# Fused attention and mixer layers on one core: one step of the float64 weight decoding moved from VectorE to ScalarE, with another order of the first 1000 pieces

## The chip, the cores and the metric

One core of one Trainium2 chip. The metric is device time in microseconds (us) of one execution of the whole program; lower is better. A core has TensorE (matrix products, into PSUM), VectorE, ScalarE and GpSimd (elementwise work) and SyncE, which here issues all transfers. Each engine takes its instructions in the order in which they were written and waits by itself for what they need. In the profile's rows TensorE is PE (its weight loads PEld), VectorE DVE, ScalarE ACT, GpSimd POOL, SyncE SP.

## What is computed

Three layers in a row, on a batch of 4 with 576 positions and 8 heads of 64 channels:

```
q_d, k_d, v_d = means over 4 positions               # 144 pooled positions
out = repeat(softmax(q_d k_d^T / 8) v_d, 4)          # pooled attention
    + softmax(band(q k^T / 8, |i - j| < 4)) v        # local attention
x = out as (4, 576, 512)

h = relu(x @ w_in)                                   # 512 -> 1024
c = sum over k of conv_w[k] * h shifted by k - 1
x = (h * sigmoid(c)) @ w_out                         # 1024 -> 512

u = x + ((x^T @ U) @ V)^T                            # along the positions, rank 32
y = u + relu(u @ w_ch1) @ w_ch2                      # 512 -> 2048 -> 512
```

The activations and q, k, v are float32. The weights (`w_in`, `conv_w`, `w_out`, `U`, `V`, `w_ch1`, `w_ch2`) arrive as float64, since numpy scales them with a float64 factor. They are read as pairs of 32-bit words and decoded on the chip.

## The kernel before, in words

The program is one list of some 2900 words, `SEQ`. Each word names a piece of work and its indices ("S.3.2": scores of pair 3 in PSUM slot 2), `ACTS` maps the name to a function, and the last loop of the kernel runs the list from left to right. Nothing else sets the order: every engine's queue is the list with the other engines' work left out, and SyncE's transfers stand in it too.

The stages overlap. The 16 pairs of (two heads) of attention are the words up to about 1060: sums over four positions (`sums`, L357), scores (L396, L462), maxima, exponentials, row sums, norms, transposes and the products with v (L530, L538), then `add_x` (L557). At the same time the 16 tiles of the first layer's weights are loaded and decoded, and the first layer starts: `g1` (L721), `relu1`, `conv_first`, `conv_rest` (L748), `tanh`, `gate` (L759), `gate_hi` and `gate_lo` (ghl, L764 and L767), `g2` (L775). The second layer's rank-32 mixing follows (L799, L820). The last layer multiplies with seven products per block of two by two (`product`, L927): `p_copy` (L932) and `p_add` (L936) bring the sums of PSUM banks together, `relu3_hi` and `relu3_lo` (L943, L947) split the result in two parts for `g4` (L959). `p_copy` reads a bank to which the next product of the block adds, so that product waits for it. The pieces "f" and the ones that `scores` adds issue matmuls whose result nobody reads (`beat`, L332).

A weight tile is 128 x 512 values, 128 x 1024 words. `w_load` brings it, `w_dec` decodes it in four steps, written as "wd.layer.tile.step" and placed in the list one by one. `dec` (L577) has the steps. With `hi` and `lo` the two words of each value (every second word of the tile) and `d` the 32 bits of the float32 that is made:

- step 0, ScalarE, L585: the high word read as a float32 and multiplied by 2^-112, into `wval`;
- step 1, VectorE, L587: `d` shifted left by 3;
- step 2, VectorE, L589: the low word shifted right by 29 (its upper three bits), or `d`;
- step 3, VectorE, L592: the sign bit of the high word, or `d`.

Then `w_hi` (ScalarE, L605) and `w_lo` (GpSimd or VectorE, L608) split the value in two reduced-precision parts for TensorE; the last layer makes sums of halves of `wval` instead (L849, L861, L865). The same `dec` decodes the convolution's weights (`cw`, 24 values a row) and U and V (`uvr`). 48 tiles are decoded: 16 of the first layer between 22 and 109 us, 32 of the last between 279 and 441 us.

Of the kernel before, what the change touches and what calls it, by code (L numbers as in the profile page):

```python
# [11 lines left out]
AF = mybir.ActivationFunctionType  # L12
ALU = mybir.AluOpType
# [5 lines left out]
SEQ = ("lq.1 xz sf sp.1 k sp.0 K qs.1 sp.1 S.1.1 lc cw.0 z M.1 lq.0 qs.0 qd.1 Sd.1.0 dp.1 lr.0 E.1 R.1 S.0.2 M.0 vs.0.0 "  # L19
# [196 lines left out]
P = 128  # L216
# [4 lines left out]
def mixer_kernel(ctx, tc, consts, qk, vw_, vr_, w1, w2, cw_, u_, v_, out):  # L221
    nc = tc.nc
    B, S, DM = out.shape
    NCC = DM // P
    NPAIR = qk.shape[0]
    D = P // 2
# [12 lines left out]
    Z = 2 if w1.dtype == U64 else 1  # L239
# [11 lines left out]
    px = tc.alloc_tile_pool(name="px", bufs=1, side="right", reuse_waits="tile")  # L251
# [325 lines left out]
    def dec(raw, dst, step, eng=nc.vector):  # L577
# [5 lines left out]
        d = dst.bitcast(U32)  # L583
# [483 lines left out]
```

## Time and profile before

| | |
|---|---|
| runs, us | 720.1, 720.26, 720.46; median 720.26 |
| the profiled execution | 715.93 us, span of its instructions 714.1 us |
| PE busy | 695.5 us (97%), 5809 matmuls |
| DVE busy | 450.7 us (63%), 790 instructions |
| ACT busy | 353.3 us (49%), 811 instructions |
| POOL busy | 207.1 us (29%), 209 instructions |
| mean granted clock of TensorE | 0.994 |
| transfers | 96.42 MB, mean 135 GB/s |

The profiled execution is one run of its own; its time is 4.3 us below the median of the others, and its rows add up to its own time. Busy is the union of an engine's instructions over the span; a busy TensorE is not TensorE at its peak, since matmuls are pipelined. A share over the whole span is a mean over stages that are bound by different things, so the stretches are read one by one. The granted clock is the share of full speed that TensorE was given.

### The profile page before, as it was taken

Reading aid. Unit: us, or ns where it says so; the run is one execution under the profiler, and the core shown is the slowest. Engines: PE = TensorE matmul, PEld = TensorE weight load, DVE = VectorE, ACT = ScalarE, POOL = GpSimd, SP = SyncE. Lnnn points to the kernel's source line nnn. Section 1 sums busy time; section 2 is a strip of 40 time slices with the busy share of each in tenths; the row PEclk is TensorE's granted clock in tenths of the full one; section 3 lists DMA queues with packets and bytes.
Section 4 is the critical chain, followed back from the end, with each engine's and each line's share of the span. In section 5 each row is a group of like instructions: output and inputs, shape, how many; then the busy total and the mean of one; then the engine's idle time right before and its main releaser. Section 6 shows DMA issues by size and latency. Waiting matters only on the chain.

```text
span 714.1 us, 14638 instructions
## 1 busy us (share of the span) xinstructions
PE 695.5 (97%) x5809; PEld 616.3 (86%) x5809; DVE 450.7 (63%) x790; ACT 353.3 (49%) x811; POOL 207.1 (29%) x209
## 2 busy tenths in 40 slices
PE   8888999999999999999999999999999999999997
PEld 6677879888889898988899988888898989998896
DVE  5999998867666466899899888832222273222223
ACT  4776877665457466787455555521221262221221
POOL 2366555444523454383332334200000020000000
PEclk9999999999999999999999999999999999999999
DMA  7988542221100000245666858454334426344312
GB/s 213 312 272 293 158 138 68 73 79 57 41 2 1 1 0 30 92 160 207 233 224 222 280 172 286 158 147 122 114 108 133 105 75 220 118 133 118 104 44 89
DMA packets 40579, 96.42 MB, mean 135 GB/s; under 512 B 4672, under 2 KB 5184, under 8 KB 40512
## 3 DMA queue, kind: packets, MB, share of 16 engines
q1 hardware_dynamic: 40512, 95.50, 41.8%
q8 instruction: 46, 0.75, 0.4%
q14 instruction: 21, 0.17, 0.1%
HBM read 76.08 MB, written 19.40 MB: 134 GB/s over the span
## 4 chain that ended last, share of the span: by engine, by line
PE 86%; DVE 9%; DMA 2%; issue 1%; ACT 1%; SPq 0%; POOL 0%; DVEq 0%; ACTq 0%
PE acc L959 26%; PE g L927 25%; PE g L721 14%; PE acc L775 13%; DMA vr<-in_vr_dram 2%; DVE wval L589 1%; PE h L799 1%; PE O L530 1%; DVE wval L592 1%; PE S L396 1%; PE O L538 1%; PE Sd L462 1%; PE Td L503 1%; PE mx L820 1%; DVE g L748 1%
## 5 line engine op out<-in xcount | busy, mean ns | idle before, releaser
L959 PE MATMUL acc<-w,a 128*128 128x512 f32 x864 | 218.6, 393 | 0.0
L927 PE MATMUL g<-bt,as 128*128 128x384 f32 x1008 | 194.7, 338 | 0.0
L927 PEld LDWEIGHTS g<-bt,as 128*128 128x128 f32 x1008 | 178.9, 188 | 10.5 <-ACT tp L932 0.7
L959 PEld LDWEIGHTS acc<-w,a 128*128 128x128 f32 x864 | 159.9, 188 | 26.2
L721 PE MATMUL g<-xhl,w 128*128 128x386 f32 (+1 forms) x576 | 117.5, 347 | 3.2 <-DVE ghl L767 3.2
L775 PE MATMUL acc<-w,ghl 128*128 128x512 f32 x432 | 112.1, 396 | 0.0
L721 PEld LDWEIGHTS g<-xhl,w 128*128 128x128 f32 x576 | 102.6, 191 | 8.6 <-DVE ghl L767 3.9
L936 DVE TENSOR_TENSOR tp<-g,tp 128x384 f32<-128x384 f32 x72 | 40.0, 556 | 100.6 <-ACT tp L932 61.7
L775 PEld LDWEIGHTS acc<-w,ghl 128*128 128x128 f32 x432 | 79.4, 188 | 14.3 <-issue 0.6
L932 ACT ACTIVATE tp<-g 128x384 f32<-128x384 f32 x72 | 35.2, 489 | 96.1 <-PE g L927 96.1
L943 ACT ACTIVATE a<-tp 128x384 fp32r<-128x384 f32 x72 | 37.7, 525 | 81.2 <-PE acc L959 57.5
L947 DVE SCALAR_TENSOR_TENSOR a<-tp,a 128x384 fp32r<-128x384 f32 x72 | 41.8, 581 | 56.6 <-ACT a L943 56.0
L748 DVE SCALAR_TENSOR_TENSOR g<-h,cw,g 128x384 f32<-128x384 f32 x96 | 59.4, 619 | 22.5 <-ACT g L743 21.1
L767 POOL TENSOR_TENSOR ghl<-ct,ghl 128x384 fp32r<-128x384 f32 x40 | 41.6, 1041 | 64.3 <-ACT ghl L764 64.3
L916 POOL TENSOR_TENSOR bt<-vb,bt 128x384 fp32r<-128x384 f32 x13 | 13.3, 1028 | 141.4 <-ACT bt L912 136.9
L608 POOL TENSOR_TENSOR w<-wval,w 128x512 fp32r<-128x512 f32 x26 | 34.6, 1332 | 57.4 <-ACT w L605 57.4
L589 DVE SCALAR_TENSOR_TENSOR wval<-raw,wval 128x512 uint32<-128x512 uint32 x48 | 38.5, 801 | 0.8
L592 DVE SCALAR_TENSOR_TENSOR wval<-raw,wval 128x512 uint32<-128x512 uint32 x48 | 37.7, 790 | 0.8
L764 ACT ACTIVATE ghl<-ct 128x384 fp32r<-128x384 f32 x40 | 20.9, 522 | 27.3 <-PE acc L775 25.0
L727 ACT ACTIVATE h<-g 128x386 f32<-128x386 f32 (+1 forms) x48 | 23.6, 491 | 21.7 <-PE g L721 21.6
L943 ACT ACTIVATE a<-g 128x384 fp32r<-128x384 f32 x24 | 11.8, 492 | 42.0 <-PE acc L959 29.9
L585 ACT ACTIVATE wval<-raw 128x512 f32<-128x512 f32 x48 | 31.5, 666 | 1.1 <-DVE w L608 1.0
(129 smaller groups left out, 849.8 us busy)
## 6 DMA issues: line engine op xcount, KB each, us to landing
as<-s SPq DMA_DIRECT2D x112, 256.0 KB, 2.7
raw<-in_w_dram SPq DMA_DIRECT2D x48, 512.0 KB, 4.9
s<-as SPq DMA_DIRECT2D x56, 256.0 KB, 2.9
qk<-in_qk_dram SPq DMA_DIRECT2D x16, 576.0 KB, 5.4
vw<-in_vw_dram SPq DMA_DIRECT2D x16, 384.0 KB, 5.0
vr<-in_vr_dram SPq DMA_DIRECT2D x16, 288.0 KB
out_dram<-u SPq DMA_DIRECT2D x17, 256.0 KB, 3.6
uvr<-in_v_dram SPq DMA_DIRECT2D x1, 576.0 KB
```

Source lines behind the costliest of these rows:

```text
L589: eng.scalar_tensor_tensor(out=d, in0=lo, scalar=29, in1=d, op0=ALU.logical_shift_right, op1=ALU.bitwise_or)
L592: eng.scalar_tensor_tensor(out=d, in0=hi, scalar=0x80000000, in1=d, op0=ALU.bitwise_and, op1=ALU.bitwise_or)
L721: nc.tensor.matmul(gp[n][:, :wd], w[:, a, cc], xhl[g, cc][:, b, :wd], start=cc == 0 and i == 0, stop=cc == NCC - 1 and i == 2)
L748: nc.vector.scalar_tensor_tensor(out=o, in0=inner(g, hts[n], k), scalar=cw[:, k * NF + f:k * NF + f + 1], in1=o, op0=ALU.mult, op1=ALU.add)
L767: eng.tensor_tensor(ghl[n][:, 1], cts.pop(n), ghl[n][:, 0].bitcast(F32), op=ALU.subtract)
L775: nc.tensor.matmul(acc[g][c], t[:, a, c * P:(c + 1) * P], w[:, b], start=f == 0 and i == 0, stop=f == NF - 1 and i == 2)
L927: nc.tensor.matmul(o, w[:, a, k], Bs[r, j, k][:, b, :TB], start=j in (0, 1, 3) and n == 0, stop=n == 3 * HC - 1, skip_group_check=True)
L932: nc.scalar.activation(out=t[:, :TB], in_=bank[q, 0][:, :TB], func=AF.Copy)
L936: nc.vector.tensor_tensor(t, bank[q, 1][:, :TB], t, op=ALU.add)
L943: nc.scalar.activation(out=t[:, 0], in_=r_src(q, k), func=AF.Relu)
L947: nc.vector.scalar_tensor_tensor(out=t[:, 1], in0=r_src(q, k), scalar=0.0, in1=t[:, 0].bitcast(F32), op0=ALU.max, op1=ALU.subtract)
L959: nc.tensor.matmul(acc2[g][c], t[:, a, c * P:(c + 1) * P], w[:, b], start=f == 0 and n < 2 and i == 0, stop=f == NFP - 1 and n >= 2 and i ...
```

## The change

`dec` makes the three bits of the low word on ScalarE: step 1 becomes an ACTIVATE in place on the low words, read as integers, scaled by 2^-29 (a little less) and shifted by -0.5 (a little more), and rounded to an integer as it is written. Step 2 on VectorE then shifts `d` by 3 and ors the three bits in one instruction. So a tile has two ScalarE and two VectorE steps, where it had one and three.

```diff
@@ dec @@
         if step == 0:
             nc.scalar.activation(out=dst, in_=hi.bitcast(F32), func=AF.Copy, scale=2.0 ** -112)
         elif step == 1:
-            eng.tensor_scalar(out=d, in0=d, scalar1=3, scalar2=None, op0=ALU.logical_shift_left)
+            nc.scalar.activation(out=lo, in_=lo, func=AF.Copy, scale=2.0 ** -29 * (1 - 2.0 ** -18),
+                                 bias=-0.5 + 7.5 * 2.0 ** -18)
         elif step == 2:
-            eng.scalar_tensor_tensor(out=d, in0=lo, scalar=29, in1=d,
-                                           op0=ALU.logical_shift_right, op1=ALU.bitwise_or)
+            eng.scalar_tensor_tensor(out=d, in0=d, scalar=3, in1=lo,
+                                     op0=ALU.logical_shift_left, op1=ALU.bitwise_or)
@@ SEQ @@
-SEQ = ("lq.1 xz sf sp.1 k sp.0 K qs.1 sp.1 S.1.1 lc cw.0 z M.1 lq.0 qs.0 qd.1 Sd.1.0 dp.1 lr.0 E.1 R.1 S.0.2 M.0 vs.0.0 "
+SEQ = ("lq.1 sf sp.0 sp.1 sp.1 k K lq.0 S.1.1 M.1 lq.2 S.0.2 z wm qs.1 qd.1 Sd.1.0 qs.0 qd.0 lc dp.1 E.1 M.0 dp.0 Sd.0.1 "
...
```

The list holds the same 2928 words. The first 1000 stand in another order; the 1928 behind them (from "re.15 r.15 Vd.14" on, in the middle of the first layer) are the same, word for word, and the step 1 of the last layer's 32 tiles keeps its places in the list, now in ScalarE's queue. In the changed file the lines up to `dec` are one lower (L584 is step 0 there, L586 the new step 1, L589 and L592 are steps 2 and 3).

VectorE at the first weight tile, before (`wval` is the decoded tile, `raw` the words, `nm`, `sm` and `P` belong to attention):

```order
L467 TENSOR_REDUCE nm<-Sd 96x3
L587 TENSOR_SCALAR wval<-wval 128x512
L589 SCALAR_TENSOR_TENSOR wval<-raw,wval 128x512
L411 TENSOR_REDUCE nm<-S 128x12
L592 SCALAR_TENSOR_TENSOR wval<-raw,wval 128x512
L450 RECIPROCAL sm_104<-sm_104 128x15
L418 TENSOR_TENSOR P<-S,nm 128x2x3x64
```

and with the change:

```order
L466 TENSOR_REDUCE nm<-Sd 96x3
L589 SCALAR_TENSOR_TENSOR cw<-cw,craw 128x24
L440 TENSOR_REDUCE sm_104<-P 128x12
L589 SCALAR_TENSOR_TENSOR wval<-wval,raw 128x512
L592 SCALAR_TENSOR_TENSOR wval<-raw,wval 128x512
L449 RECIPROCAL sm_104<-sm_104 128x15
```

The shift of L587 is gone, and a row sum of attention and a step of `cw` stand ahead of the tile's two steps.

ScalarE in the last layer, in the part of the list that is unchanged, where three tiles are decoded between the copies of `tp` (L932, `p_copy`; `a` is L943, `relu3_hi`):

```order
-L585 ACTIVATE wval_5375<-raw_5294 128x512
-L585 ACTIVATE wval_5381<-raw_5319 128x512
+L584 ACTIVATE wval_5375<-raw_5294 128x512
+L584 ACTIVATE wval_5381<-raw_5319 128x512
+L586 ACTIVATE raw_5294<-raw_5294 128x512
 L932 ACTIVATE tp_5387<-g_5368 128x384
-L585 ACTIVATE wval_5395<-raw_5325 128x512
+L586 ACTIVATE raw_5319<-raw_5319 128x512
+L584 ACTIVATE wval_5395<-raw_5325 128x512
 L943 ACTIVATE a_5404<-tp_5387 128x384
+L586 ACTIVATE raw_5325<-raw_5325 128x512
 L932 ACTIVATE tp_5415<-g_5368 128x384
```

Two ACTIVATEs more stand ahead of L943, and three ahead of the second `tp`.

## Rows read from the trace of the kernel before

**Rows 1.** The page: the chain of waits, shares of the span by engine.
```profile
PE 86%; DVE 9%; DMA 2%; issue 1%; ACT 1%; SPq 0%; POOL 0%; DVEq 0%; ACTq 0%
```

**Rows 2.** Windows: stretch, length, busy PE, PEld, DVE, ACT, POOL (instructions), clock, DMA, GB/s.
```profile
0.00:20.00 20.00, 17.03 (x401) 12.72 (x401) 12.66 (x23) 9.57 (x30) 5.99 (x16) 1.00 0.77 215
20.00:65.00 45.00, 36.69 (x784) 32.66 (x778) 43.29 (x72) 31.58 (x90) 22.24 (x19) 0.92 0.88 290
65.00:85.00 20.00, 20.00 (x303) 17.60 (x301) 17.10 (x30) 17.07 (x41) 11.33 (x11) 1.00 0.71 227
85.00:105.00 20.00, 18.34 (x328) 15.25 (x327) 19.79 (x35) 14.22 (x34) 10.96 (x10) 1.00 0.43 121
105.00:440.00 335.00, 335.00 (x2661) 299.36 (x2659) 261.65 (x459) 206.91 (x467) 146.04 (x146) 1.00 0.33 113
440.00:705.00 265.00, 263.75 (x1327) 235.12 (x1327) 91.95 (x169) 73.40 (x151) 10.48 (x10) 1.00 0.41 123
705.00:714.10 9.10, 4.70 (x21) 3.57 (x19) 4.23 (x8) 0.52 (x1) 0.00 (x0) 0.92 0.48 173
```

**Rows 3.** Timeline of TensorE: start, length, what, and idle time before.
```profile
29.05 1.06 PE L332 MATMUL O<-mask,identR 128*128 128x224 f32 x7 [2.83 <-DVE xd L548]
...
60.50 1.87 PE L721 MATMUL g<-xhl,w 128*128 128x386 f32 x5 [2.73 <-DVE ghl L767]
```

**Rows 4.** Windows of 5 us behind these two idle times.
```profile
30.00:35.00 5.00, 4.70 (x150) 4.17 (x152) 4.33 (x9) 4.11 (x11) 0.20 (x1) 0.67 0.94 287
60.00:65.00 5.00, 4.50 (x16) 4.33 (x17) 5.00 (x11) 2.44 (x6) 2.05 (x2) 0.66 0.94 280
```

**Rows 5.** Chain of waits to 125 us: start, length, what.
```profile
23.19 0.42 DVE wval L587
...
32.28 0.68 ACT wval L585
...
40.09 1.56 DVE wval L587 x2
...
60.50 3.93 PE g L721 x12
...
91.27 0.34 DVE wval L587
...
121.67 2.15 PE g L721 x12
```

**Rows 6.** Groups of instructions from 20 to 105 us: busy us, mean ns, idle.
```profile
L589 DVE SCALAR_TENSOR_TENSOR wval<-raw,wval 128x512 uint32<-128x512 uint32 x15 | 14.0, 935 | 0.2
...
L587 DVE TENSOR_SCALAR wval<-wval 128x512 uint32<-128x512 uint32 x16 | 7.3, 466 | 0.7 <-ACT wval L585 0.7
...
L585 ACT ACTIVATE wval<-raw 128x512 f32<-128x512 f32 x16 | 10.7, 667 | 0.1
```

**Rows 7.** Timeline of GpSimd, then of VectorE, at 57 to 60 us.
```profile
57.42 2.01 POOL L486 TENSOR_TENSOR vr<-vr 72x512 f32<-72x512 f32 x1 [1.61 <-DVE g L759]
...
58.34 1.64 DVE L589 SCALAR_TENSOR_TENSOR wval<-raw,wval 128x512 uint32<-128x512 uint32 x1
```

**Rows 8.** Timelines at 400 to 406 us: ScalarE, then TensorE.
```profile
400.47 1.22 ACT L585 ACTIVATE wval<-raw 128x512 f32<-128x512 f32 x2
401.71 0.49 ACT L932 ACTIVATE tp<-g 128x384 f32<-128x384 f32 x1
402.10 0.66 ACT L585 ACTIVATE wval<-raw 128x512 f32<-128x512 f32 x1
403.08 0.53 ACT L943 ACTIVATE a<-tp 128x384 fp32r<-128x384 f32 x1 [0.32 <-PE acc L959]
404.14 0.49 ACT L932 ACTIVATE tp<-g 128x384 f32<-128x384 f32 x1 [0.53 <-PE g L927]
...
402.88 3.33 PE L927 MATMUL g<-bt,as 128*128 128x384 f32 x18
```

**Rows 9.** Groups of the whole span: ScalarE's longest ACTIVATE.
```profile
L650 ACT ACTIVATE Us<-uvr 128x960 fp32r<-128x960 f32 x1 | 1.0, 990 | 0.0
```

387 rows, old and new, of the table SEQ are left out of this document.

## The prediction

> **What bounds the kernel now.** Read first the shares of the chain of waits: 86% of it is TensorE and 9% VectorE [rows 1]. TensorE is the floor, and a change on other engines can save only what TensorE stands idle or runs slowly. Next, the windows tell where that is [rows 2]. From 105 to 440 us TensorE is busy for all 335.00 us, and from 440 to 705 us for 263.75 of 265.00; nothing can be won there, only lost. From 0 to 20 us it misses 2.97 us (start-up). From 20 to 105 us it misses 45.00 - 36.69 + 20.00 - 18.34 = 9.97 us, and in the same 85 us VectorE is busy for 43.29 + 17.10 + 19.79 = 80.18 us, ScalarE for 62.87. So this stretch, in which attention and the decoding of the 16 tiles of the first layer run together, is VectorE's. The timeline of TensorE names the two longest idle times, 2.83 us behind a VectorE copy of `xd` and 2.73 us behind VectorE's first `ghl` [rows 3]. After each the granted clock falls: 0.67 and 0.66 over the next 5 us, a mean of the levels 2.4 and 1.2 GHz, so some 3.3 of the 5 us at the lower [rows 4]; twelve matmuls of L721 then take 3.93 us where later ones take 2.15 [rows 5]. That second price is 1.8 us.
>
> **What the change does, part by part.**
>
> *The shift that goes.* Each float64 tile loses VectorE's TENSOR_SCALAR of L587. Sixteen run between 20 and 105 us, 466 ns each, 7.3 us busy [rows 6]. What of it set the end is read from the chain: 0.42, 1.56 for two together and seven pieces of 0.33 to 0.35 (one of them shown), 0.42 + 1.56 + 7 x 0.34 = 4.4 us [rows 5]. I take 4.4. The bounds are 7.3 (every one on the path) and 0 (VectorE would then wait for something else). The other 32 tiles are decoded at 280 to 440 us, where TensorE is never idle: their relief is worth nothing, and so is that of the small `cw` and `uvr` decodes.
>
> *Busy time against chain.* Some of these shifts and of the two-input operations behind them are long: the one at 58.34 took 1.64 us while GpSimd's L486 ran from 57.42 for 2.01 us [rows 7], and L589 averages 935 ns in this stretch [rows 6]. The double shift of 1.56 us is such a case too. Taking the shift out does not take GpSimd's operation away; the next VectorE operation meets it. So I count the chain pieces and not the busy time. The Trainium skill ("SBUF — State Buffer", section Who interferes with whom) says why: a VectorE copy-like operation in its two-port modes, or one with two SBUF inputs, and a GpSimd operation that reads SBUF hold the shared port pair against each other for a whole instruction. By that rule the 7.3 us would not all come back; the long one at 58.34 agrees with it.
>
> *TensorE's clock.* The order of instructions on VectorE shows 83 ahead of the first `ghl` (L767) before and 76 now: nine of L587 fewer, two others more. At 0.34 us and more for each of the nine, VectorE comes there some 3 us earlier, against an idle time of 2.73 us [rows 3]. I count this idle time as closed and the slow clock behind it as gone: 1.8 us. The idle time at 29 us has only two of L587 ahead of it, and stays. Bounds: 0, and 3.4 with both.
>
> *The ScalarE operation that comes.* No row shows an ACTIVATE from uint32 to uint32 in place with a step of two. The nearest is L585, the same engine, 512 elements, the other half of the same words: 667 ns [rows 6], 0.66 for the one at 402.10 [rows 8]. I take 0.67. The lower end is 0.6 (the two at 400.47 took 1.22 together [rows 8]); the upper end, twice the row, 1.33, if integers cost extra; the longest ACTIVATE in the trace is 990 ns for 960 elements [rows 9]. Sixteen more are 10.7 us in a stretch where ScalarE is busy 62.87 of 85 us, and its idle 22 us hold them. Where VectorE stands at the step behind, the tile's own path grows by 0.67 - 0.41 = 0.26 us. Before, VectorE waited there once (the chain passes through ScalarE's L585 at 32.28, 0.68 us [rows 5]); I count two tiles, +0.5.
>
> *The swapped operands of step 2* read the same two tiles, so L589 keeps its time: 0.
>
> *The list to piece 1000.* It holds the same pieces, and TensorE's work is unchanged. Ahead of the scores of pair 9 TensorE has 1699 matmuls in both orders, and VectorE 153 instructions before and 135 now; L587 makes 17 of the 18 (16 tiles and `cw`). So the list moves work about rather than out of the stretch: 0, with bounds of -2.8 and +2.8, one of the long idle times closed or opened [rows 3]. No queue is passed by a transfer in a way that I can price; loads count in a rival.
>
> *The list behind piece 1000.* It is as before, but 32 ACTIVATEs of 0.67 us now stand in ScalarE's queue there. I followed ScalarE's rows from 280 to 440 us, pushed by 0.6 us (start to start) at each and relieved by each idle time. One place reaches TensorE: at 400 to 404 us three insertions stand among the copies of `tp`. The copy at 404.14 moves by 0.6 + 0.6 - 0.32 + 0.6 - 0.53 = 0.95 us [rows 8], to 405.6; the product that overwrites its bank is the last third of the 18 matmuls that start at 402.88 and take 3.33 us, so at 402.88 + 2.22 = 405.1. That is 0.5 to 0.6 us of stall: +0.6. VectorE's step 2 comes up to 1.4 us late at five tiles, and no TensorE start stood that close behind. Bounds: 0 and 3.
>
> **Sum:** -4.4 - 1.8 + 0.5 + 0.6 = -5.1 us. The profiled execution took 715.93 us (span 714.1), so 710.8; the median of the runs is 720.26, 4.3 us above it, so **715.2** there.
>
> **Rivals.**
>
> *ScalarE takes VectorE's place (slower).* For it: with 10.7 us more ScalarE is busy 73.6 of 85 us, in order, and VectorE's two remaining steps wait for both ScalarE steps. If the added 0.67 us stands in VectorE's way at half of the 16 tiles, the sum is 8 x 0.67 - 4.4 + 0.6 = +1.6 us, **721.8**; at all of them +6.9, 727.2. It decides from six tiles on, 6 x 0.67 = 4.0 against 4.4 - 0.6. Against it: the chain passes once through L585 in the stretch, and in the new order the second ACTIVATE mostly stands one or two instructions behind the first, with other VectorE work between. The Trainium skill ("ScalarE: Activation LUTs", section Rules for kernel authors) speaks for this rival: adds and multiplies belong on VectorE. The rows agree as far as they go, 667 ns against 466 for the step; by that rule alone the 16 tiles cost 3.2 us more engine time, 723.5.
>
> *Transfers hold it (no change).* The DMA engines are busy 0.88 of 20 to 65 us, and 0.94 in both slow stretches [rows 2, 4]. If the tiles come no earlier, VectorE's relief there becomes waiting; only the four shifts of 85 to 105 us count, 4 x 0.34 = 1.4, and 1.4 - 0.5 - 0.6 leaves **720.0**. Against it: hardly any wait in the stretch ends on a transfer; the ones named are VectorE's.
>
> *More than the sum.* All sixteen shifts on the path and both slow stretches gone: -7.3 - 3.4 = -10.7, **709.6**.
>
> **How the numbers follow.** The forecast's own case has 0.58, the larger gain 0.08, the transfers 0.13, ScalarE 0.21. What a measurement can tell from no change is 0.2%, 1.4 us. Faster 0.66, same 0.13, slower 0.21. The range goes from 710.0, near the larger gain, to 722.0, which takes in ScalarE at half of the tiles; the forecast's case by itself lies in 711 to 718.5.
>
> **What would show it.** Right: no L587 on VectorE, 50-odd ACTIVATEs of some 0.67 us on ScalarE; VectorE near 73 of the 85 us, TensorE's idle time from 20 to 105 us down from 9.97 to some 6 us, no slow clock near 60 us; from 280 to 440 us less than 1 us idle. Wrong: TensorE waits in the first 105 us that end on ScalarE or on VectorE's L589 behind ScalarE, an ACTIVATE well over 0.7 us, or several stalls at 300 to 440 us that end on the copies of `tp`.

## The result, and the profile after

The changed kernel takes 724.26 us (median of four, 722.79 to 724.44) where the kernel before takes 720.18 (median of four, 719.34 to 720.46): 4.1 us more by these medians. The ratio of the two, on which the rest of this text builds, is 1.0071, 95% interval 1.0046 to 1.0097, or 5.1 us slower; it is not the quotient of the two medians, which is 1.0057. Ratios leave out executions of over 1.5% above the fastest of the same kernel, which among the later versions were one each in three (2951.95 us of the hoisted kernel, 725.22 us of the one with pair 0 first, 727.49 us of the changed one without step 1). The forecast was 715.2, the range 710.0 to 722.0. The profiled execution took 724.26 us, its span is 722.4.

The page, shares of the chain of waits by engine, and two groups of instructions over the whole span:

```profile
PE 78%; DVE 11%; ACT 5%; DMA 3%; issue 2%; POOL 0%; SPq 0%; DVEq 0%; ACTq 0%
...
L589 DVE SCALAR_TENSOR_TENSOR wval<-wval,raw 128x512 uint32<-128x512 uint32 x48 | 36.0, 750 | 12.1 <-ACT raw L586 7.9
...
L586 ACT ACTIVATE raw<-raw 128x512 uint32<-128x512 uint32 x48 | 32.0, 666 | 0.0
```

ScalarE's new ACTIVATE takes 666 ns, and VectorE's step 2 now waits for it, 7.9 us over the span, nearly all of it in the last layer. ScalarE's share of the chain is 5% where it was 1% [rows 1]. The windows, with the columns of [rows 2], and then five stretches of 5 us:

```profile
0.00:20.00 20.00, 12.96 (x242) 9.20 (x242) 9.02 (x15) 7.27 (x25) 4.32 (x14) 0.99 0.73 220
20.00:65.00 45.00, 38.63 (x898) 33.21 (x896) 33.06 (x58) 31.73 (x87) 16.79 (x17) 0.81 0.77 252
65.00:85.00 20.00, 18.33 (x246) 16.02 (x247) 16.69 (x28) 16.42 (x41) 10.39 (x9) 1.00 0.42 128
85.00:105.00 20.00, 19.94 (x257) 17.59 (x258) 17.51 (x30) 18.52 (x48) 13.83 (x14) 1.00 0.62 220
105.00:440.00 335.00, 333.54 (x2788) 296.37 (x2788) 249.22 (x426) 223.94 (x502) 143.75 (x144) 1.00 0.33 112
440.00:705.00 265.00, 263.62 (x1328) 235.17 (x1327) 95.00 (x172) 76.71 (x160) 14.95 (x16) 1.00 0.43 130
```
```profile
20.00:25.00 5.00, 3.82 (x130) 3.33 (x132) 3.41 (x5) 2.31 (x5) 1.88 (x3) 0.69 0.71 219
40.00:45.00 5.00, 3.64 (x37) 2.55 (x31) 3.74 (x7) 4.20 (x14) 2.99 (x4) 0.86 0.97 292
45.00:50.00 5.00, 4.50 (x115) 3.53 (x111) 4.06 (x9) 2.10 (x5) 1.68 (x2) 0.50 0.92 289
50.00:55.00 5.00, 4.77 (x66) 4.10 (x66) 0.22 (x2) 2.14 (x10) 1.86 (x2) 0.50 0.92 310
55.00:60.00 5.00, 5.00 (x28) 4.94 (x27) 4.47 (x7) 3.54 (x9) 1.37 (x2) 0.78 0.46 136
```

Against the rows of before [rows 2] TensorE's idle time grew by 17.03 - 12.96 = 4.07 us in the first 20 us, fell by 1.87 from 20 to 105 us (45.00 - 38.63 + 20.00 - 18.33 + 20.00 - 19.94 = 8.10, from 9.97), and grew by 1.46 from 105 to 440 us. Its busy time is 700.3 us in place of 695.5 for the same 5809 matmuls; that is the lower clock. From 45 to 55 us it was granted 0.50, the level of 1.2 GHz, without a break, and from 50 to 55 us VectorE was busy for 0.22 of 5 us: it waited 4.8 us for ScalarE's copy `xd` of what the slow matmuls made. The new place of loss is the start. The chain of waits from 12 to 20 us (start, length, what):

```profile
12.98 0.73 PE Sd L461 x6
13.71 1.57 PE S L331 x14
15.28 0.02 issue
15.30 0.49 ACT P L435
15.79 0.72 ACT Pd L473 x5
...
16.66 1.29 ACT Pd L473 x7
...
17.97 0.32 ACT sm L445
...
18.31 0.26 DVE sm L449
...
18.64 0.84 POOL P L454
...
19.52 0.81 PE T L495 x3
```

Fourteen matmuls of L331, whose result nobody reads ("f.14"), stand on the chain, and all that TensorE does next hangs on what ScalarE starts behind them. They write spare columns of the very tile S that ScalarE's `exps` of pair 0 (E.0) reads, and the new list has f.14 ahead of E.0; the old list had it behind. ScalarE and then TensorE on the timeline:

```profile
15.30 0.49 ACT L435 ACTIVATE P<-S 128x384 f32<-128x384 f32 x1 [2.20 <-PE S L331]
```
```profile
13.45 1.81 PE L331 MATMUL S<-mask,identR 128*128 128x224 f32 x14
19.52 0.81 PE L495 MATMUL T<-front,P 128*128 128x128 f32 x3 [4.26 <-POOL P L454]
```

In the kernel before it is the beats that wait, 0.97 us for ScalarE's `P`, and the same piece T.0.1 (L496 there) starts 2.8 us earlier:

```profile
13.74 1.93 PE L332 MATMUL S<-mask,identR 128*128 128x224 f32 x15 [0.97 <-ACT P L436]
...
16.75 0.55 PE L496 MATMUL T<-front,P 128*128 128x128 f32 x3
```

### The profile page after: what moved, and what is told of

Read it like the earlier page. It is cut to its first block, busy times and chain, and to the rows that moved or that the text cites. A ratio compares the mean times of both kernels' runs of the same rounds, so it can differ in the third digit from the quotient of the medians.

```text
span 722.4 us, 14631 instructions
## 1 busy us (share of the span) xinstructions
PE 700.3 (97%) x5809; PEld 618.8 (86%) x5809; DVE 427.4 (59%) x739; ACT 377.1 (52%) x862; POOL 204.0 (28%) x209
## 4 chain that ended last, share of the span: by engine, by line
PE 78%; DVE 11%; ACT 5%; DMA 3%; issue 2%; POOL 0%; SPq 0%; DVEq 0%; ACTq 0%
PE acc L959 22%; PE g L927 21%; PE acc L775 11%; PE g L721 11%; DMA raw<-in_w_dram 2%; DVE wval L592 2%; DVE wval L589 2%; PE S L395 2%; PE O L529 1%; DVE g L748 1%; PE O L537 1%; PE Sd L461 1%; PE h L799 1%; PE Td L502 1%; ACT raw L586 1%
## 5 line engine op out<-in xcount | busy, mean ns | idle before, releaser
L927 PE MATMUL g<-bt,as 128*128 128x384 f32 x1008 | 195.7, 338 | 1.1 <-ACT tp L932 0.6
L927 PEld LDWEIGHTS g<-bt,as 128*128 128x128 f32 x1008 | 178.5, 188 | 13.2 <-ACT tp L932 2.7
L775 PE MATMUL acc<-w,ghl 128*128 128x512 f32 x432 | 113.9, 397 | 0.0
L932 ACT ACTIVATE tp<-g 128x384 f32<-128x384 f32 x72 | 35.0, 487 | 90.0 <-PE g L927 89.9
L943 ACT ACTIVATE a<-tp 128x384 fp32r<-128x384 f32 x72 | 37.6, 524 | 78.2 <-PE acc L959 55.6
L589 DVE SCALAR_TENSOR_TENSOR wval<-wval,raw 128x512 uint32<-128x512 uint32 x48 | 36.0, 750 | 12.1 <-ACT raw L586 7.9
L592 DVE SCALAR_TENSOR_TENSOR wval<-raw,wval 128x512 uint32<-128x512 uint32 x48 | 36.2, 759 | 1.0
L759 DVE SCALAR_TENSOR_TENSOR ct<-g,h 128x384 f32<-128x384 f32 x40 | 22.1, 553 | 19.5 <-ACT g L752 13.8
L584 ACT ACTIVATE wval<-raw 128x512 f32<-128x512 f32 x48 | 31.7, 668 | 3.7 <-DMA raw<-in_w_dram 3.2
L586 ACT ACTIVATE raw<-raw 128x512 uint32<-128x512 uint32 x48 | 32.0, 666 | 0.0
```

The costliest lines, as they stand in the source:

```text
L586: nc.scalar.activation(out=lo, in_=lo, func=AF.Copy, scale=2.0 ** -29 * (1 - 2.0 ** -18), bias=-0.5 + 7.5 * 2.0 ** -18)
L589: eng.scalar_tensor_tensor(out=d, in0=d, scalar=3, in1=lo, op0=ALU.logical_shift_left, op1=ALU.bitwise_or)
L592: eng.scalar_tensor_tensor(out=d, in0=hi, scalar=0x80000000, in1=d, op0=ALU.bitwise_and, op1=ALU.bitwise_or)
L775: nc.tensor.matmul(acc[g][c], t[:, a, c * P:(c + 1) * P], w[:, b], start=f == 0 and i == 0, stop=f == NF - 1 and i == 2)
L927: nc.tensor.matmul(o, w[:, a, k], Bs[r, j, k][:, b, :TB], start=j in (0, 1, 3) and n == 0, stop=n == 3 * HC - 1, skip_group_check=True)
L943: nc.scalar.activation(out=t[:, 0], in_=r_src(q, k), func=AF.Relu)
```

## The experiments

Each is timed against the kernel before on the same chip; the runs stand on three chips, and the changed kernel itself was timed four times and not again beside them. A ratio has an interval of about 2 us to either side, and a difference of two ratios one of 2.4 to 4 us. Theory in short: the decoding is worth what was forecast and the list loses it. Rivals: ScalarE's added step loses it; late loads lose it; TensorE's clock alone does.

### The two halves apart

The kernel before once more, to see how far one execution's rows are from another's:

> The kernel before once more, for a second profile of it. The first profiled execution took 715.93 us and the timed ones 719.3 to 720.5. If that gap is chance, a second profile shows about 720 us and names where the 4 us lie: either more of the 1.2 GHz stretch in the first 105 us (about 4 us lost there), or something behind it. If the first profile is the rule, 716 us again.

718.9 us in its one execution, span 717.1. On this chip 13 executions of before lie between 716.47 and 720.28, median 717.72; the profile of [rows 1 to 9] is below the lowest of them, so the 4 us are largely chance.

The new `dec` with the old list, and the old `dec` with the new list:

```diff
@@ decoding alone: dec as in the change; SEQ as before
@@ order alone: dec as before; SEQ as in the change
```

> The changed decoding with the old list of pieces. Theory A (the new order of the first 1000 pieces costs the time, the decoding itself relieves VectorE): 714 to 718 us, faster than before, with the last layer's stalls of about 1 us in it. Theory B (the second ScalarE step stands in VectorE's way, whatever the order): 724 us or more, with waits of VectorE's L589 on ScalarE's L586 in the first 105 us.

> The old decoding (one ScalarE and three VectorE steps) with the new list. Theory A: 724 us or more, since the idle time of 4.3 us at 15 to 20 us and the long stretch at 1.2 GHz are the list's, and VectorE has its shifts on top: 724 to 730. Theory B: about 720, as before.

Decoding alone: 719.85 us, ratio 1.0028 (1.0000 to 1.0057). Order alone: 732.1, ratio 1.0211 (1.0169 to 1.0254). Neither half gains, and both fall outside their theories' numbers: 719.85 lies between A and B, 732.1 above even A's range. The halves do not add up either: 2.0 and 15.2 us apart, 5.1 together. In the new list the new decoding is worth 1.0211 - 1.0071 = 1.40%, 10.1 us, so the new list suits the new decoding and not the old. With the order alone TensorE's start is the changed kernel's (busy 12.95 of the first 20 us), and the granted clock from 20 to 65 us is 0.74; why the old decoding loses so much more there was not followed. With the decoding alone VectorE is busy 6.4 us less than before from 20 to 105 us (39.03 + 18.16 + 16.64 = 73.83, from 80.18), and TensorE's idle time there is no shorter, 11.73 us against 9.97. Windows of the order alone (one) and of the decoding alone (three), then VectorE's waits with the decoding alone from 20 to 105 us (total, times, longest):

```profile
20.00:65.00 45.00, 34.19 (x817) 30.02 (x816) 31.17 (x55) 22.80 (x66) 15.15 (x15) 0.74 0.64 203
```
```profile
20.00:65.00 45.00, 36.41 (x824) 32.26 (x816) 39.03 (x64) 35.58 (x98) 20.40 (x19) 0.96 0.87 292
65.00:85.00 20.00, 19.51 (x283) 16.87 (x264) 18.16 (x29) 19.30 (x47) 11.96 (x11) 1.00 0.66 213
85.00:105.00 20.00, 17.35 (x323) 14.70 (x324) 16.64 (x29) 16.08 (x37) 10.01 (x10) 1.00 0.40 110
```
```profile
DVE wval L590 <- issue: 2.9, 2, 2.4
DVE wval L590 <- ACT raw L587: 2.1, 3, 1.3
```

The 2.4 is put down to "issue"; the timelines of VectorE and ScalarE show what it is:

```profile
93.18 0.69 DVE L590 SCALAR_TENSOR_TENSOR wval<-wval,raw 128x512 uint32<-128x512 uint32 x1 [2.44 <-issue]
```
```profile
91.86 0.67 ACT L585 ACTIVATE wval<-raw 128x512 f32<-128x512 f32 x1
92.43 1.23 ACT L587 ACTIVATE raw<-raw 128x512 uint32<-128x512 uint32 x2
```

VectorE starts as the first of ScalarE's two L587 ends: the word that was VectorE's shift in the old list is ScalarE's now, at the same place, behind the exponentials of a pair and another tile's step 0.

### What the removal is worth, and what ScalarE's step costs

Old list, step 1 left out, so that the decoded values lack their true low bits; then old list, each step 1 of the first layer put right behind its step 0 (four of the 16 stood there already):

```diff
@@ without step 1 @@
-            nc.scalar.activation(out=lo, in_=lo, func=AF.Copy, scale=2.0 ** -29 * (1 - 2.0 ** -18),
-                                 bias=-0.5 + 7.5 * 2.0 ** -18)
+            pass
...
-                                     op0=ALU.logical_shift_left, op1=ALU.bitwise_or)
+                                     op0=ALU.logical_shift_left, op1=ALU.bitwise_and)
@@ hoisted, SEQ, for all 16 tiles k @@
-wd.1.k.0
+wd.1.k.0 wd.1.k.1
...
-wd.1.k.1
```

> The new decoding in the old list, with ScalarE's step 1 left out: the low word's three bits are not made, and step 2 takes d shifted by 3 and the low word together (an and in place of the or), so the decoded values lack their true low bits. VectorE has one step less and ScalarE nothing more. This prices the removal by itself. Forecast's step: the removal alone is worth 4.4 us or more (ratio 0.994). Theory 'ScalarE gives the relief back': 3 us or more below the decoding alone. Theory 'clock': TensorE's idle times and slow stretches take most of the relief even so, and the ratio is 0.998 to 1.002.

> The new decoding in the old list, with each step 1 of the 16 tiles of the first layer put right behind its step 0, so that ScalarE makes the three bits long before VectorE asks for them. In the run with the new decoding alone VectorE waited 4.8 us for ScalarE's step 1 (2.44 us of it at one tile at 90.7 us). Theory 'ScalarE gives the relief back': these waits go, TensorE's idle time from 20 to 105 us falls by 2 us or more, and the time is some 2 to 3 us below the decoding alone, about 1 to 2 us below the kernel before (ratio 0.997). Theory 'clock': the relief does not reach the end, since the idle times move rather than go and each is followed by a slow stretch in some executions; the ratio to before stays at 1.000 to 1.004.

Without step 1: 714.11, ratio 0.9924 (0.9900 to 0.9948), 5.5 us faster. Hoisted: 717.77, ratio 0.9979 (0.9956 to 1.0003), 1.5 us faster. So the removal by itself is worth 5.5 us; ScalarE's step costs 1.0028 - 0.9924 = 1.04%, 7.5 us, where the old list puts it, and 0.55%, 4.0 us, where it is made early. With the hoisting VectorE waits next to nothing for step 1 (0.3 us, from 5.0 with the decoding alone), but the rest of ScalarE's work comes later. The windows of the whole stretch, without step 1 and hoisted:

```profile
20.00:105.00 85.00, 78.42 (x1440) 68.95 (x1432) 77.30 (x128) 66.71 (x175) 47.28 (x42) 0.98 0.73 239
```
```profile
20.00:105.00 85.00, 73.76 (x1428) 64.05 (x1419) 71.98 (x119) 71.15 (x180) 43.53 (x38) 0.98 0.75 234
```

TensorE idles 6.6 us in the one and 11.2 in the other, at the same granted clock; the theory of the hoisted run asked for 2 us less than the 11.73 of the decoding alone, and the profile shows 0.5 less. Of the difference between the two, 3.2 us are stops of TensorE that nothing released (4.6 us hoisted, 1.4 without step 1; the last section tells of them); of the other 1.4 us the largest part is a wait for ScalarE's `qd` (1.5 us hoisted, 0.3 without step 1). The 4.0 us rest on the timed runs, not on these two profiles.

The same step left out of the changed kernel, in the new list:

> The changed kernel, new list, with ScalarE's step 1 left out: the low word's three bits are not made, and step 2 takes d shifted by 3 and the low word together (an and in place of the or), so the decoded values lack their true low bits. In the old list the same step cost 7.5 us (1.0028 against 0.9924). Theory 'the new list hides ScalarE's step and loses at the start': the ratio falls little, to 1.002 to 1.006, since the start's loss stays and the step stands early in every tile. Theory 'ScalarE is the cost in both lists': the ratio falls by about 1%, to 0.996 to 0.999.

720.09, ratio 1.0015 (0.9988 to 1.0042). It lies between the two theories: the step costs 1.0071 - 1.0015 = 0.56%, 4.0 us, in the new list, as much as in the hoisted order. And the list, with ScalarE's step out of the comparison, costs 1.0015 - 0.9924 = 0.91%, 6.6 us. So the result splits into -5.5 + 4.0 + 6.6 = +5.1 us. That the terms add up is no test of them: each is the difference of two neighbours in one row of ratios. Nor is the list's price one number: it is 15.2 us with the old decoding, 6.6 without step 1, and 1.0071 - 1.0028 = 0.43%, 3.1 us, with the new decoding, whose step 1 costs less there than in the old list.

### What in the list costs it

S.2.1 put ahead of T.0.1, so that TensorE has scores to make in the 4.26 us; the three loads that SyncE holds back behind lr.3 put ahead of it; and 24 more of the matmuls that nobody reads, in the idle time:

```diff
@@ S.2.1 first @@
-T.0.1 re.1 S.2.1
+S.2.1 T.0.1 re.1
@@ loads first (the three stood behind, with other words between) @@
-lr.3
+wl.1.2 lw.1 lw.2 lr.3
@@ more beats @@
-f.14
+f.38
```

> The changed kernel with one piece moved: the scores of pair 2 stand ahead of pair 0's transposes on TensorE, as in the old list, so that TensorE has about 2 us of work while GpSimd norms pair 0. Theory A1 (the idle time of 4.3 us at the start and the slow clock behind it make the loss): 2 to 4 us less than the changed kernel, 720 to 722. Theory A2 (the start is hidden by later waits for VectorE; the loss is the slow clock at 43 to 57 us and its cause): within 1 us of the changed kernel, 724.

> The changed kernel with three loads of SyncE's queue (wl.1.2, lw.1, lw.2) put ahead of lr.3. In the changed kernel's trace SyncE issues nothing from 19.4 to 28.45 us, where lr.3 waits for the buffer of vd of pair 1, and the three loads behind it come up to 9 us late. Theory 'late loads': these loads are what VectorE and TensorE wait for at 40 to 56 us, and the time falls by 3 us or more, to some 721. Theory 'clock': the loads are not what is waited for; the slow stretch of TensorE at 43 to 57 us stays and the time stays within 1.5 us of the changed kernel's 724.

> The changed kernel with 24 more matmuls whose result nobody reads (f.14 becomes f.38) in the 4.26 us in which TensorE stands idle at 15.3 to 19.5 us; they take some 3.1 us by the 14 before them (1.81 us), and end ahead of what T.0.1 waits for. No wait is taken away, and no work is moved. Theory 'clock': the slow stretch at 19.7 to 23.1 us follows the idle time; with the idle time filled it is gone, what comes behind is 1 to 2 us earlier, and the time falls by 1 us or more. Theory 'order': the time is set by what VectorE, ScalarE and the loads deliver; nothing changes, or the matmuls stand in the way, and the time stays at 724 or grows.

None of the three helped: 727.33 (ratio 1.0103, 1.0047 to 1.0159), 726.94 (1.0102, 1.0050 to 1.0153) and 724.52 (1.0091, 1.0059 to 1.0124). Loads are not it: the three left SyncE by 25.4 us in place of 28.8 to 33.5, and a gain of 3 us lies outside the interval. The third showed what makes the start late: the idle time did not get filled, it moved, and with 24 more beats T.0.1 came 3.4 us later. (The whole run grew by 1.0091 - 1.0071 = 0.2%, 1.4 us with an interval of some 3 to either side, so a late start need not reach the end in full.) ScalarE in that run, then TensorE:

```profile
18.66 0.49 ACT L439 ACTIVATE P<-S 128x384 f32<-128x384 f32 x1 [4.88 <-PE S L335]
```
```profile
14.13 4.49 PE L335 MATMUL S<-mask,identR 128*128 128x224 f32 x38
22.89 0.90 PE L499 MATMUL T<-front,P 128*128 128x128 f32 x3 [4.27 <-POOL P L458]
```

E.0 waits for the beats: 2.20 us with 14 of them, 4.88 with 38. Hence one word moved, and then with it the order of the two pairs:

```diff
@@ beats behind E.0 @@
-f.14 cw.0 Md.0 E.0 Ed.1 Ed.0 R.0
+cw.0 Md.0 E.0 f.14 Ed.1 Ed.0 R.0
@@ and pair 0 first @@
-E.0 f.14 Ed.1 Ed.0 R.0 qs.2 R.1 re.0 r.0 n.0 lq.3 qd.2 T.0.1 re.1 S.2.1
+E.0 f.14 Ed.0 R.0 qs.2 re.0 r.0 n.0 Ed.1 R.1 lq.3 qd.2 S.2.1 T.0.1 re.1
```

> The changed kernel with one word moved: f.14, 14 matmuls whose result nobody reads, from ahead of E.0 to right behind it, as it stands in the old list. They write spare columns of the tile that E.0 reads; in the changed kernel ScalarE's E.0 waits 2.20 us for them (13.1 to 15.3 us), and with 24 more of them it waited 4.88 us and T.0.1 came 3.35 us later. Theory 'beats in the way': E.0 starts at some 13.1 us, T.0.1 at 17.7 in place of 19.52, and the time falls by 1.5 to 3 us, to 721 to 723. Theory 'clock': the start is shorter, but another idle time and slow stretch follows; the time stays within 1.5 us of 724. If the idle time at the start decides all, the ratio to before comes to 1.002 or less.

> As the run with the beats behind E.0, and besides Ed.1 and R.1 moved from ahead of Ed.0 to behind n.0, and S.2.1 to ahead of T.0.1, so that ScalarE serves pair 0, for which TensorE waits, before pair 1, and TensorE has scores to make meanwhile. By the rows of the changed kernel T.0.1 starts at 17.0 us (before: 16.75). Theory 'order at the start': all of the start's 2.5 to 3 us come back, the time is 720 to 721.5. Theory 'clock': the first 20 us come back, but the slow stretches at 40 to 60 us stay, and the time is 723 to 727 as in the run with S.2.1 moved alone.

Beats behind E.0: 720.4, ratio 1.0024 (0.9990 to 1.0058). With pair 0 first: 716.11, ratio 0.9967 (0.9933 to 1.0002). One word gave back 0.47%, 3.4 us, and the order of the pairs, with S.2.1 ahead of T.0.1, 0.57%, 4.1 us, each with an interval of 3 to 3.5 us to either side. Together they are 7.5 us (4.4 to 10.6), more than was expected of them, and as much as the list's loss of 6.6 within the intervals: with its first words put right the new list is within the intervals as fast as the old one with step 1 hoisted (0.9967 against 0.9979). T.0.1 starts at 17.41 and 17.48 us in place of 19.52, and in the second run TensorE has its scores behind it by then:

```profile
13.84 1.94 PE L335 MATMUL S<-mask,identR 128*128 128x224 f32 x15
15.61 0.37 PE L392 MATMUL S<-mask,identR 128*128 128x192 f32 x2
15.91 1.00 PE L399 MATMUL S<-qk 64*24 64x32 f32 x96
17.48 0.55 PE L499 MATMUL T<-front,P 128*128 128x128 f32 x3 [0.56 <-POOL P L458]
```
```profile
20.00:65.00 45.00, 36.19 (x806) 31.60 (x797) 33.20 (x59) 31.58 (x90) 18.62 (x17) 0.92 0.86 280
```

7.5 us are more than the 2 us by which T.0.1 comes earlier. The rest goes with TensorE's clock: in the changed kernel's profile 0.69 from 20 to 25 us, right behind the start's idle time, and 0.81 over the 45 us; in the pair-0 run 0.92 over the same 45 (the window above). The timed runs agree: a mean granted clock of 0.986 to 0.988 in the changed kernel's four, 0.989 to 1.000 in the pair-0 run's eleven. How a longer start leads to the lower level at 45 to 55 us, 20 us later, stays open; right ahead of it TensorE stopped for 0.97 us without a releaser (last section).

### The same beats elsewhere, and the best version

The 2.83 us of idle time at 26 us in the kernel before [rows 3] are of the same kind: seven beats (f.7) write into a tile `O` from which VectorE's `xdv.1` must first read. In the hoisted kernel f.7 was put ahead of that reader, behind Vd.1; then qd.4 ahead of tile 1's two ScalarE steps as well; and f.7 alone in the kernel before:

```diff
@@ f.7 ahead of xd @@
-Vd.1 r.2 D.3 nv.2 Md.3 xdv.1 wl.1.2 nd.2 lq.4 wo.1.0 qs.4 f.7
+Vd.1 f.7 r.2 D.3 nv.2 Md.3 xdv.1 wl.1.2 nd.2 lq.4 wo.1.0 qs.4
@@ and qd.4 @@
-wd.1.1.0 wd.1.1.1 qd.4
+qd.4 wd.1.1.0 wd.1.1.1
```

> The run with step 1 hoisted in the old list, with one word more moved: f.7 from behind xdv.1 to right behind Vd.1. The seven matmuls write spare columns of the tile from which xdv.1 reads, and in that run TensorE waits 2.48 us for VectorE's xdv.1 before them, at 27.6 us; the kernel before has the same wait, 2.83 us. Theory 'beats in the way': the seven run at 27.6 us at once, T.2.0 follows when its own operands are there, some 1 us earlier, and the slow stretch behind is rarer; the time is 1 to 3 us below the hoisted run's 717.77, ratio to before 0.994 to 0.997. Rival: T.2.0 waits for VectorE's norm of pair 2 anyway, which ends at 29.3 us, and xdv.1 now waits for the seven; the time is as in the hoisted run.

> The hoisted run with f.7 ahead of xd, and qd.4 moved ahead of the two ScalarE steps of tile 1. There TensorE waited 2.49 us at 31.0 us for qd.4, which stood behind c.2, cd.2 and tile 1's two ACTIVATEs of 0.68 us. If ScalarE's queue is what keeps the removal's full worth from the end, qd.4 and Sd.4.0 come 1.1 us earlier and the time falls by 0.5 to 1.1 us, ratio 0.993 to 0.995. Rival: the next wait takes its place, and the ratio stays at 0.996.

> The kernel before, old decoding and old list, with only f.7 moved from behind xdv.1 to right behind Vd.1. It tells how much of the 0.9958 of the hoisted run with the same move belongs to the beats' place and not to the new decoding. If the beats' place alone does it: ratio 0.996 or less, and the new decoding is worth nothing in the old list. If the new decoding with step 1 hoisted is worth the 1.5 us that the hoisted run showed: ratio 0.998 to 1.000 here.

Hoisted with f.7 moved: 715.42, ratio 0.9958 (0.9934 to 0.9981), 3.0 us below the kernel before and the only one that computes everything and whose interval lies below 1. With qd.4 moved too: 717.76, ratio 0.9984 (0.9959 to 1.0008), no further gain: it holds the same move of f.7, and came out 0.26% higher, so part of the 0.9958, the best of many runs, may be luck; the wait for qd.4 fell from 2.49 to 1.39 us and two others grew in its place (1.16 us on VectorE's `P`, 1.69 instead of 1.15 at the first `g` that waits for `ghl`). f.7 alone in the kernel before: 0.9989 (0.9970 to 1.0009). So most of the 0.9958 seems to need the new decoding with its step made early, but the intervals overlap, and the move of f.7 is by itself worth nothing that these runs can show, in the hoisted kernel (0.9979 to 0.9958) or in the one before. TensorE in the hoisted kernel, without and with f.7 moved:

```profile
30.08 1.04 PE L335 MATMUL O<-mask,identR 128*128 128x224 f32 x7 [2.48 <-DVE xd L551]
```
```profile
26.98 1.04 PE L335 MATMUL O<-mask,identR 128*128 128x224 f32 x7
28.79 0.55 PE L499 MATMUL T<-front,P 128*128 128x128 f32 x3 [0.77 <-DVE P L458]
```

## Why the prediction was wrong

- **The shift that goes, -4.4, and TensorE's clock, -1.8:** right together in the old list. Without the shift and with nothing in its place the kernel is 5.5 us faster (3.7 to 7.2); the wait at the first `ghl` fell from 2.73 us [rows 3] to 1.1 in that run (first line under this list), and the granted clock from 20 to 105 us was 0.98. To count chain pieces and not the 7.3 us of busy time was the right choice, as 7.3 + 1.8 = 9.1 lies outside that interval. In the changed kernel the clock's term failed. The wait at the first `ghl` is gone, as forecast, but not because VectorE comes there some 3 us earlier: it comes at 70.4 us and not at 59.9. The lower clock stands at 45 to 55 us instead, and TensorE's busy time grew by 4.8 us.
- **The ScalarE operation that comes, +0.5:** its duration was right (0.67 forecast, 666 ns measured), its place was not. The prediction's step was that ScalarE's idle 22 us hold it and that VectorE stands behind it at two tiles. It cost 7.5 us in the old list and 4.0 in the new: about eleven and six of the operations. ScalarE's queue is in order and serves attention too, so an operation that VectorE no longer waits for can still push back what TensorE waits for. In the hoisted profile that is `qd` (1.5 us, 0.3 without step 1); which waits make up the rest of the 4.0 us the profiles do not show. The rival "ScalarE takes VectorE's place" had this as a matter of VectorE's waits alone. The Trainium skill ("ScalarE: Activation LUTs", section Rules for kernel authors) puts multiplies and adds on VectorE. This case agrees only in part: in the old list the move costs 2.0 us on balance (7.5 against the 5.5 won), made early it wins 1.5 (4.0 against 5.5), and neither is clear of noise.
- **The list to piece 1000, 0 (bounds -2.8 to +2.8):** this step failed most, with 6.6 us. I counted instructions ahead of a mark on TensorE and VectorE and found the sums equal. I didn't follow who reads the tile that the beats write, nor the order of pairs on ScalarE in the first 20 us, since the profile of before has no long wait there: its beats wait 0.97 us for the very reader behind which they stand, and its start missed 2.97 us, the new one 7.04. The bounds of 2.8 us came from the idle times at 29 and 60 us, not from the start. What the runs showed in place of the 0 is a start that f.14 and the order of the pairs make late, with the lower clock behind it; moved back, they gave 7.5 us.
- **The list behind piece 1000, +0.6:** as forecast in the changed kernel's trace, one wait of 0.60 us of L927 on the copies of `tp` (second line under this list); in the trace of the decoding alone it was absent, so it is 0 to 0.6. Two waits of 0.4 and 0.3 us on `ct` were not foreseen.
- **Busy time and idle time:** VectorE came to 33.06 + 16.69 + 17.51 = 67.3 us of the 85, forecast 73; TensorE's idle time to 8.1, forecast 6. Work of attention and of one tile more had been pushed past 105 us by the longer start, so VectorE's smaller number is no gain.

```profile
PE g L721 <- DVE ghl L767: 1.1, 1, 1.1
```
```profile
PE g L927 <- ACT tp L932: 0.6, 1, 0.6
```

## What to carry to other kernels

An operation that goes to an engine with idle time is not free: its price is what stands behind it in that engine's queue and is waited for, and it is measured by leaving it out (5.5 us) and by making it early (a price of 4.0 in place of 7.5). Matmuls that only keep TensorE busy write somewhere; a list that puts them ahead of a reader of the same tile makes them work that is waited for, and one that puts them behind makes them wait. When an order is changed, follow the first microseconds word by word on every engine, also where the old profile shows no long wait. And an order has no price of its own: this one cost 15.2 us with the old decoding and 3.1 with the new.

## What the runs showed of the hardware

**TensorE stops at fixed counts of its own instructions.** Some of its idle times had no releaser ("issue") and mostly lay in the middle of a row of equal matmuls. In the 16 profiles of this study every such stop of over 0.3 us behind the first 8 us, 41 in all, came at one of six places, counted in matmuls that TensorE had executed: 349, 475, 603, 730 (once 729), 857 and 984 or 985, that is 126 to 128 apart. With one weight load for each that is some 255 instructions, whatever the operation was. At number 857, in 15 of the 16, the hoisted kernel shows:

```profile
41.00 0.44 PE L499 MATMUL T<-front,P 128*128 128x128 f32 x2 [1.20 <-issue]
```

the changed kernel, behind a stop at number 349:

```profile
24.68 0.92 PE L529 MATMUL O<-PT,vw 64*64 64x48 f32 x48 [1.18 <-issue]
...
43.56 1.12 PE L461 MATMUL Sd<-ss,qd 128*96 128x144 f32 x4 [0.97 <-issue]
```

the changed kernel with 24 matmuls more ahead of it, where the count fell on other work:

```profile
45.41 0.68 PE L533 MATMUL O<-PT,vw 64*64 64x48 f32 x15 [2.48 <-issue]
```

and the new list with the old decoding:

```profile
50.06 0.77 PE L461 MATMUL Sd<-ss,qd 128*96 128x144 f32 x4 [3.29 <-issue]
```

They took 0.3 to 3.3 us each and 1.05 to 5.4 us in a profile (1.05 in the kernel before, 2.6 in the changed one), all between 23 and 52 us, where the transfers of data are dense (DMA engines busy for 0.71 to 0.97 in the changed kernel's windows). The page of each profile has a queue of the kind "instruction" with 46 packets:

```profile
q8 instruction: 46, 0.75, 0.4%
```

That is 16 KB a packet, and 5809 matmuls with as many weight loads make 45.4 blocks of 256. By the start times in the traces TensorE went on 1.2 to 1.7 us after the end of such a packet, at all 41 stops; in the changed kernel a packet ended at 42.08 us, and the stop at 43.56. So TensorE waited there for its own instructions. The Trainium skill ("Runtime: NRT & Kernel Launch", section Instruction fetch mechanics) says that an engine's instructions are fetched by DMA in blocks of 256, mostly hidden. The count and the packets agree with these blocks; here some were not hidden. That the data's transfers delay them was not tried.

**One kernel's executions differ by TensorE's clock.** Of the run with pair 0 first, three executions with a granted clock of 1.00 took 712.9 to 713.5 us, and three at 0.989 to 0.991 took 719.8 to 722.4. In the profiles most of the lower level of 1.2 GHz lies between 20 and 65 us. What a version is worth by its median is thus also how often an execution falls to that level, and a single profile can be 4 us off its own median, as the one that the prediction was built on.
